# Retention and a routed expert layer in one kernel: four positions of k and v to a packet, chunks of 128 positions on 32 partitions, a mask built by VectorE, and a shifted start in the order model

## The chip, the cores and the metric

The kernel runs on one core of a Trainium2 chip. The metric is the device time of one execution in microseconds, lower is better. Engines are named as in the profile: PE is TensorE (PEld its weight loads), DVE is VectorE, ACT is ScalarE, POOL is GpSimd and SP is SyncE, which here only issues transfers.

## The reference

Eight heads of decayed attention (retention) over 8 sequences of 576 positions, then a layer of eight experts of which each row takes two:

```python
scores = scale * np.matmul(q, k.transpose(0, 1, 3, 2))
gamma = 1.0 - 2.0 ** (-5.0 - np.arange(H))
Dmat = np.where(rel >= 0, gamma[:, None, None] ** rel[None, :, :], 0.0)
attn_out = np.matmul(scores * Dmat[None], v)          # (8, 8, 576, 64)
x = attn_out.transpose(0, 2, 1, 3).reshape(4608, 512)
noisy_logits = x @ w_gate + np.log1p(np.exp(x @ w_noise)) * noise
...
h = np.maximum(x[mask] @ w1[e], 0.0)
out[mask] += top2_w[mask, k, None] * (h @ w2[e])
```

q, k and v are 8 x 8 x 576 x 64 in float32, w1 is 8 x 512 x 1024, w2 is 8 x 1024 x 512.

## The kernel before

**The attention part.** The work is cut into 16 units. A unit is one sequence and four heads; four units make a group `bp` of two sequences. Of the 576 positions the first 512 belong to the unit, and the 64 of the end (the "tail") are done once for each group. The decay is put into q and v by tables (`tab`, `tabq`), so that a chunk of positions needs only a mask of zeros and ones, and what earlier chunks give comes through a state, the sum of k times v over them. For each unit the steps are: `load` (q, k, v from HBM into float32 tiles), `cast` (scale to bf16: k on ACT, q and v on POOL or DVE), `tr` (eight transposes each of k and q on PE, copied back by ACT or DVE), `scores` (k times q inside each of four chunks of 128 positions, evicted by DVE through the mask), `states` (the four running states, evicted into a block-diagonal tile `tb`), and `out_` (the part inside the chunk, `intra`, and the part from the states, `inter`, evicted into `xT`, which holds the rows of x transposed).

**How positions lie.** k and v are loaded in two halves of 256 positions, and in each half partition p holds the positions 2p and 2p+1, so one row of a packet is 2 x 64 numbers of 4 bytes, 512 bytes. A chunk then covers 64 partitions. `scores` and `intra` make 16 matmuls for each pair of heads, with 64 partitions of operand and 64 columns of weights, so that four of them stand side by side in the array. `states` makes 32 matmuls: 16 over 64 partitions and 16 over 128. The transfer of k covers 4 to 16 heads, two transfers for k and two for v each time; from the second group on they bring the data of two units at once. q comes in packets of 2048 bytes, the tail's in packets of 256 bytes.

**The routing and the experts.** After each group, `tail` and `route` compute logits, the two best experts and a place for each row, and write x in rows to HBM (`xd`). The rows are gathered from there for the experts (POOL, indirect transfers), multiplied by w1 and w2 on PE, and scattered to the output (POOL). Some blocks of rows are final before all groups are routed: these "early tiles" (`up`, L1101, and `second`, L1189) are run between the units. All other blocks go through `wide` (L1127) and `second` when the attention is over. The weights of the first three experts come through POOL's transfers, those of the other five through SP's.

**What sets the order.** Nothing runs in the order of the code. `record` lists the operations with their tiles, and `Plan.run` goes through a model with a cost for each operation, takes the one that can start first, and gives it the tiles; each engine's instructions are then written out in that order and run strictly in it. The numbers in the calls of `pl.op` are these costs. SP's loads go through `inp`, which lets a load go only after the load five before it has landed. Where the model sees PE idle before an operation that takes a PSUM tile, `warm` puts matmuls of no use into that tile beforehand (L298), `o.fill` of them, to keep PE at work. They run on the identity and the mask and so need both. Of the eight PSUM tiles the attention may hold seven.

## Time and profile before

| what | us |
|---|---|
| median of 3 runs | 424.81 |
| lowest and highest run | 424.1, 427.77 |
| profiled execution, its own time | 423.66 |
| its span, first to last instruction | 422.1 |
| PE busy in the span | 380.5 |
| ACT, POOL, DVE busy | 265.2, 289.5, 157.8 |
| transfers over the span | 95.92 MB, mean 227 GB/s |

The page of the profile gives busy times by engine, the span in 40 slices, transfers by queue, and groups of instructions by line. Beside it stand answers about the trace: busy times in stretches (columns: stretch, its length, then the busy us and the number of instructions of each engine, the granted clock of PE as a share, the busy share of the 16 DMA engines, and GB/s), instructions in order of time (start, duration, engine, line, operation, tiles, count), and groups of instructions by shape. A DMA share can be over 1 where transfers of two queues overlap on an engine.

### The profile page before, as it was taken

How to read it: one execution, taken by the hardware profiler on the slowest of the kernel's cores; microseconds unless marked ns; L12 is line 12 of the kernel's file. 1: busy time of each engine (PE TensorE's matmuls, PEld its weight loads, DVE VectorE, ACT ScalarE, POOL GpSimd, SP SyncE). 2: the span in 40 equal slices, each digit the busy share in tenths (PEclk: the TensorE clock that was granted, in tenths of full speed). 3: DMA queues.
4: the chain of work that ended last, by engine and by line, in shares of the span. 5: the costliest groups of instructions: out<-in, count | busy, mean ns of one | idle time of the engine just before them, and what ended most of it. 6: DMA issues, size and time to landing. Idle time of an engine off the chain costs nothing. (4 is left out here: it accounts for less than half of the span.)

```text
span 422.1 us, 11266 instructions
## 1 busy us (share of the span) xinstructions
PE 380.5 (90%) x4418; PEld 243.4 (58%) x4418; DVE 157.8 (37%) x459; ACT 265.2 (63%) x459; POOL 289.5 (69%) x314
## 2 busy tenths in 40 slices
PE   4996774986998888999999999999999999999992
PEld 3875654875876666666566644554554454454451
DVE  4645489688858859201232412021121100000001
ACT  2797674983987776556666756655755754555550
POOL 8774594793498827666477677776776786783673
PEclk9999895998999999999999999999999999999998
DMA  7996999999999999943668899999999999787595
GB/s 229 310 250 156 287 315 268 299 288 228 266 318 174 268 206 277 388 143 115 219 222 299 299 199 239 300 236 292 324 224 309 200 119 153 140 117 115 67 136 96
DMA packets 105177, 95.92 MB, mean 227 GB/s; under 512 B 42015, under 2 KB 82464, under 8 KB 105122
## 3 DMA queue, kind: packets, MB, share of 16 engines
q1 hardware_dynamic: 87298, 59.33, 50.4%
q0 software_dynamic: 17824, 35.85, 41.6%
q8 instruction: 35, 0.57, 0.5%
q14 instruction: 20, 0.16, 0.2%
HBM read 72.71 MB, written 26.36 MB: 235 GB/s over the span
## 5 line engine op out<-in xcount | busy, mean ns | idle before, releaser
L1189 PE MATMUL ps<-W,half 128*128 128x512 bf16 x576 | 185.9, 380 | 0.8 <-ACT half L290 0.4
L1127 PE MATMUL ps<-big,W 128*128 128x512 bf16 (+4 forms) x640 | 181.5, 329 | 0.0
L1110 ACT ACTIVATE half<-ps 128x512 bf16<-128x512 f32 (+5 forms) x190 | 94.8, 504 | 97.2 <-PE ps L1127 76.6
L1024 POOL DMA_INDIRECT xg<-xd,xi x80 | 82.7, 1033 | 56.4 <-issue 19.6
L1233 POOL DMA_INDIRECT out_dram<-half,xg x74 | 95.0, 1284 | 32.3 <-issue 14.2
L1189 PEld LDWEIGHTS <-half 128*128 128x128 bf16 x576 | 55.6, 98 | 61.7 <-issue 0.8
L1127 PEld LDWEIGHTS <-W 128*128 128x128 bf16 x640 | 62.5, 98 | 47.8 <-issue 1.0
L1229 DVE TENSOR_SCALAR half<-ps,xg 128x512 f32<-128x512 f32 (+1 forms) x22 | 13.8, 627 | 101.4 <-PE ps L1199 54.8
L1227 ACT ACTIVATE half<-ps,xg 128x512 f32<-128x512 f32 (+1 forms) x57 | 38.1, 668 | 13.1 <-PE ps L1189 12.5
L589 DVE TENSOR_TENSOR half<-ps,mask 128x512 bf16<-128x512 f32 x64 | 40.0, 682 | 12.3 <-PE ps L581 11.6
L290 ACT ACTIVATE half<-ps 128x1024 bf16<-128x1024 bf16 (+1 forms) x36 | 34.8, 988 | 10.0 <-PE ps L556 4.9
L1101 PE MATMUL ps<-half,W 128*128 128x256 bf16 (+1 forms) x288 | 29.5, 257 | 4.6 <-DMA W<-in_moe_w_dram 3.2
L1101 PEld LDWEIGHTS <-W 128*128 128x128 bf16 x288 | 23.9, 98 | 8.2 <-DMA W<-in_moe_w_dram 3.5
L298 PE MATMUL ps<-mask,ident__61 128*128 128x256 bf16 x146 | 21.3, 296 | 7.1 <-POOL mask L361 5.9
L290 ACT ACTIVATE tb<-ps 64x512 bf16<-64x512 f32 x32 | 18.9, 589 | 6.0 <-PE ps L614 5.1
L290 ACT ACTIVATE W<-big 128x1024 bf16<-128x1024 f32 x22 | 22.4, 1048 | 0.0
L534 POOL TENSOR_TENSOR half<-big,tab 128x512 bf16<-128x512 f32 x16 | 16.7, 1051 | 6.7 <-DMA big<-in_v_dram 3.4
L298 PEld LDWEIGHTS <-ident__61 128*128 128x128 bf16 x146 | 14.9, 106 | 9.7 <-POOL ident__61 L353 4.6
L292 DVE CAST W<-big 128x1024 bf16<-128x1024 f32 x18 | 12.1, 716 | 20.4 <-PE ps L1199 15.0
L614 PE MATMUL ps<-half,half 64*64 64x64 bf16 (+2 forms) x512 | 17.2, 214 | 2.7 <-POOL half L534 2.4
L290 ACT ACTIVATE xT<-ps 128x512 bf16<-128x512 f32 (+1 forms) x37 | 18.6, 558 | 0.8 <-PE ps L659 0.5
L534 POOL TENSOR_TENSOR half<-W,tab 128x512 bf16<-128x512 f32 x16 | 17.6, 1109 | 1.8 <-DMA W<-in_v_dram 1.6
(179 smaller groups left out, 433.5 us busy)
## 6 DMA issues: line engine op xcount, KB each, us to landing
big<-in_moe_w_dram SPq DMA_DIRECT2D x40, 512.0 KB
W<-in_moe_w_dram POOLq DMA_DIRECT2D x12, 512.0 KB, 9.6
xd<-xg SPq DMA_DIRECT2D x16, 264.0 KB
W<-in_q_dram SPq DMA_DIRECT2D x16, 256.0 KB
big<-in_k_dram SPq DMA_DIRECT2D x8, 512.0 KB
big<-in_v_dram SPq DMA_DIRECT2D x8, 512.0 KB
big<-in_q_dram SPq DMA_DIRECT2D x16, 256.0 KB
W<-in_k_dram SPq DMA_DIRECT2D x6, 512.0 KB
```

Of the source, the lines that this page charges most:

```text
L290: self.nc.scalar.activation(out, in_, Act.Copy)
L298: self.nc.tensor.matmul(b.t[:, :2 * P], lhsT=ident, rhs=mask.rearrange("p r x -> p (r x)"), start=True, stop=True, skip_group_check=True)
L534: self.eng(e).tensor_tensor(o, i, t, Alu.mult)
L589: nc.vector.tensor_tensor(S.t.bitcast(BF16).rearrange("p (h c x) -> p h c x", h=2, c=2)[:, h], p[h].t.rearrange("p (c x) -> p c x", c=2), ...
L614: nc.tensor.matmul(o[h * HD:(h + 1) * HD, hp, n, :], lhsT=kk[:k, r, c, y], rhs=vv[:k, r, c, y].unsqueeze(1).to_broadcast([k, n.stop - n.st ...
L1024: ins = nc.gpsimd.indirect_dma_start(out=x.t[:n, :], out_offset=None, in_=self.xd[:rows, :], in_offset=IOff(ap=xi.t[:n, h:h + 1], axis=0), ...
L1101: nc.tensor.matmul(pv()[:, f2, :], lhsT=w.t[:, o:o + P], rhs=xv()[:, di, :n], start=(di == 0), stop=(di == KD - 1))
L1110: self.nc.scalar.activation(o, i, Act.Relu)
L1127: self.mm = nc.tensor.matmul(p.t[:, :n], lhsT=w.t[:, o:o + P], rhs=xv()[:, di, :n], start=(di == 0), stop=(di == KD - 1))
L1189: self.mm = self.nc.tensor.matmul(po.t, lhsT=hv[:, c:c + P], rhs=self.W[e].t[:, o:o + DM], start=(f == 0), stop=(f == KF - 1))
L1227: nc.scalar.activation(y.t[:n, c], x, Act.Copy, scale=g()[:n])
L1233: ins = nc.gpsimd.indirect_dma_start(out=self.out[:, :], out_offset=IOff(ap=ix()[:n], axis=0), in_=y.t[:n, :], in_offset=None, bounds_chec ...
```

## The change

**Loads.** Partition p now holds the four positions 4p to 4p+3 of k and v, so a row of a packet is 1024 bytes, and each unit has one transfer of 512 KB for k and one for v. The two transfers of q for each unit stay. A raw tile holds two units.

**Chunks on 32 partitions.** A chunk of 128 positions covers 32 partitions. `scores` and `intra` make 32 matmuls for each pair of heads, with 32 columns of weights in the one and 32 partitions of operand in the other, so that eight stand side by side. `states` makes 64 matmuls, of 128, 96, 64 and 32 partitions for the four states. `out_` takes four PSUM tiles where it took two, half filled, and has four evictions of 256 columns where it had two of 512. The cast of k is one operation of 1024 columns on ACT, not two of 512.

**Mask.** `mask` has four planes. POOL writes two index tiles (`row`, `col`), and DVE makes the planes with four comparisons; four selections on POOL go.

**Order model.** SP's first transfer ends `RAMP` = 2.0 us later in the model, all engines start at 1.0 us, long setup operations of POOL take part in the port rule, `warm` fills only after 15 us of the model's time and uses the PSUM tile that has been free longest instead of the operation's own, and some costs are new (`scores` 0.4 to 0.32, `intra` 0.45 to 0.32, `states` 0.9 to 1.2). The order of everything follows from these and from the new operations.

```diff
@@ Plan
+    RAMP = 2.0
...
-        free, dma_free, port, paced = {}, {}, [0.0], 0.0
+        free, dma_free, port, paced = dict.fromkeys(("PE", "ACT", "DVE", "POOL"), 1.0), {"SP": self.RAMP}, [0.0], 0.0
...
-            if e == "PE" and t < self.WARM and o.allocs:
-                x = max([free.get(e, 2.5)] + [y[0] for x, b in taken for y in x])
-                o.fill = max(0, int((t - x - 0.2) * 0.8 / 0.11))
+            if e == "PE" and 15.0 < t < self.WARM:
+                b = min((x for x in self.slots["ps"] if x[1] is None), key=lambda x: x[0], default=None)
+                n = b and int((t - max(free.get(e, 2.5), b[0]) - 0.2) * 0.8 / 0.11)
+                if n and n > 0:
+                    o.fill = b[2], n
@@ setup
-        mask = f("mask", [P, 2, P], BF16)
...
-                    G.affine_select(m, m, pattern=[[1, 4], [4, 2], [8, 16]], base=-r, channel_multiplier=-2,
-                                    compare_op=Alu.is_ge, fill=0.0)
+        mask = f("mask", [P, 4, P], BF16)
...
+        for r in range(4):
+            o("DVE", 0.2, (mask, r), lambda r=r: V.tensor_scalar(mask.t[:, r], col.t, thr.t, float(r), Alu.subtract, Alu.is_ge),
+              -6, r=[col, thr])
@@ load
-            m = slice(u % 4 * 4, 16 if u % 4 == 2 else 8 if bp or u else 4)
-            for c, t in enumerate(self.raw[n]):
...
-                        m, 256 * c:256 * c + 256].rearrange("h (p r) d -> p h (r d)", r=2)),
-                    w, u, 0.22 * (m.stop - m.start))
+            self.inp(lambda e, s=s, t=t, hq=hq: nc.sync.dma_start(
+                out=flat(t)[:, hq * 1024:hq * 1024 + 1024].rearrange("p (h x) -> p h x", h=4),
+                in_=s[:, :512].rearrange("h (p r) d -> p h (r d)", r=4)), [(t, hq)], u, 1.54)
@@ cast
-        for c in range(2):
-            pl.op({"ACT": 0.63}, 0, lambda e, c=c: k(e, c), r=[(rk[c], x4)], w=[(kn, c)], prio=u, port=True)
+        pl.op({"ACT": 1.06}, 0, k, r=[(rk, hq)], w=[kn], prio=u, port=True)
@@ scores
-                for c in range(2):
-                    for r in range(2):
-                        for h in range(2):
...
-                                nc.tensor.matmul(o[h][e * HD:(e + 1) * HD, c, r], lhsT=kt[s, hp, c, r, e, :],
+                for r in range(4):
+                    for h in range(2):
+                        s = slice(h * HD, (h + 1) * HD)
+                        for j in range(4):
+                            nc.tensor.matmul(o[h][j * 32:(j + 1) * 32, r], lhsT=kt[s, hp, r, j, :],
...
-            pl.op("PE", 0.4, pe, r=[K, Q], w=p, prio=u)
+            pl.op("PE", 0.32, pe, r=[K, Q], w=p, prio=u)
@@ states
-            for k, z in ((HD, 1), (P, 0)):
...
-                                nc.tensor.matmul(o[h * HD:(h + 1) * HD, hp, n, :], lhsT=kk[:k, r, c, y],
-                                                 rhs=vv[:k, r, c, y].unsqueeze(1).to_broadcast([k, n.stop - n.start, HD]),
+            for n in (3, 2, 1, 0):
+                k = 32 * n + 32
                 for hp in range(2):
+                    for r in range(4):
+                        for h in range(2):
...
+                            nc.tensor.matmul(o[h * HD:(h + 1) * HD, hp, n, :], lhsT=kk[:k, r, y], rhs=vv[:k, r, y],
...
-        pl.op("PE", 0.9, lambda e, p=p: pe(e, p), r=[kn, vn], w=[p], prio=u)
+        pl.op("PE", 1.2, lambda e, p=p: pe(e, p), r=[kn, vn], w=[p], prio=u)
@@ out_
-        p = [self.psum("att") for e in range(2)]
+        p = [self.psum("att") for j in range(4)]
...
+            for r in range(4):
+                for h in range(2):
+                    for j in range(4):
+                        q = slice(j * 32, (j + 1) * 32)
+                        nc.tensor.matmul(o[j][h * HD:(h + 1) * HD, hp], lhsT=v[q, r, 2 * hp + h, :], rhs=s[q, h, r],
...
-            pl.op({"ACT": 0.6, "DVE": 0.69}, 0, ev, r=[p[e]], w=[(xT, (hq, b, e))], prio=u)
+            pl.op({"ACT": 0.39, "DVE": 0.42}, 0, ev, r=[p[j]], w=[(xT, (hq, b, j))], prio=u)
```

**Where it moves instructions: SP at the start.** SP's first issues before (W0 to W2 are the buffers for raw q, k and v; a row with x2 stands for two issues):

```order
L485 DMA W1_123<-in_k_dram 128x4x128 x2
L475 DMA W0_122<-in_q_dram 64x2x512 x2
L485 DMA W2_124<-in_v_dram 128x4x128 x2
L485 DMA W1_123<-in_k_dram 128x4x128 x2
L475 DMA W0_122<-in_q_dram 64x2x512 x2
```

SP's first issues now:

```order
L484 DMA W1_123<-in_k_dram 128x4x256
L478 DMA W0_122<-in_q_dram 64x2x512 x2
L484 DMA W1_123<-in_v_dram 128x4x256
L484 DMA W1_123<-in_k_dram 128x4x256
L445 DMA noise_159<-in_moe_noise_dram 64x4x32 x2
L449 DMA noise_159<-in_moe_noise_dram 64x4x8
L445 DMA noise_159<-in_moe_noise_dram 64x4x32
L478 DMA W0_122<-in_q_dram 64x2x512 x2
```

Two issues of k and of v have become one each, and four of the six small loads of the noise now stand ahead of the second unit's q.

**SP at the first group's tail.** Before, the loads of the tail (the `half` tiles, 64x8x64) and of the noise stood in turn, after the v of the units 4 and 5 (big2, big3):

```order
L441 DMA noise_156<-in_moe_noise_dram 64x4x32
L485 DMA big3_80<-in_v_dram 128x8x128
L497 DMA half6_88<-in_k_dram 64x8x64
L441 DMA noise_156<-in_moe_noise_dram 64x4x32
L497 DMA half6_88<-in_k_dram 64x8x64
L445 DMA noise_156<-in_moe_noise_dram 64x4x8
L497 DMA half16_98<-in_q_dram 64x8x64
L441 DMA noise_156<-in_moe_noise_dram 64x4x32
L497 DMA half16_98<-in_q_dram 64x8x64
L441 DMA noise_156<-in_moe_noise_dram 64x4x32
L497 DMA half11_93<-in_v_dram 64x8x64 x2
L445 DMA noise_156<-in_moe_noise_dram 64x4x8
```

The same place now, after unit 4's loads (big0, W0, big1):

```order
L484 DMA big1_78<-in_v_dram 128x4x256
L494 DMA half2_84<-in_k_dram 64x8x64 x2
L432 DMA half14_96<-in_moe_w_gate_dram 128x4x8
L432 DMA half14_96<-in_moe_w_noise_dram 128x4x8
L439 DMA xd_57<-half6_88 1x264
L494 DMA half7_89<-in_q_dram 64x8x64 x2
L494 DMA half13_95<-in_v_dram 64x8x64 x2
L484 DMA big0_77<-in_k_dram 128x4x256
```

The six loads of the noise are gone from here; the two loads of the gates' weights and the write of one dummy row, which stood just ahead, have moved in.

More of the change, by code (lines that the diff above doesn't have):

```diff
@@ L245, in run @@
             if o.fill:
-                self.warm([b for b in o.allocs if b.cls == "ps"][0], o.fill)
+                self.warm(*o.fill)
             o.fn(o.on)
@@ L312, in o @@
         def o(e, cost, b, fn, prio, r=()):
-            pl.op(e, cost, lambda e: fn(), r=r, w=[b], prio=prio)
+            pl.op(e, cost, lambda e: fn(), r=r, w=[b], prio=prio, port=e == "POOL" and cost > 0.8)
         pl.op("ACT", 1.3, lambda e: nc.scalar.preload_act_table_set("natural_log_exp_and_others"), prio=-10)
@@ L463, in load @@
         d = self.u[u] = {}
-        if u % 4 == 0:
-            self.raw = {n: [pl.buf("big", "att", 2) if bp % 2 else pl.buf("wkv", "att") for c in range(2)] for n in "kv"}
-        rows = lambda t, m: (t.t.rearrange("p b x -> p (b x)") if t.n == 2 else t.t)[:, m.start * P:m.stop * P].rearrange(
-            "p (h x) -> p h x", x=P)
+        if u % 2 == 0:
+            self.raw = {n: pl.buf("big", "att", 2) if bp % 2 else pl.buf("wkv", "att") for n in "kv"}
+        flat = lambda t: t.t.rearrange("p b x -> p (b x)") if t.n == 2 else t.t
         for n in "kqv":
```

122 lines of the change are left out of this document (48 added, 74 removed).

## Prediction

> **What bounds the kernel now.** First the busy time in stretches of the span, cut where PE's work changes: the start, the first tail, the middle units, the last units with the first early tiles, the early tiles after the last unit, the wide blocks, the end.
>
> ```profile
> core 0: us, PE busy (x) PEld busy (x) DVE busy (x) ACT busy (x) POOL busy (x), PEclk, DMA share, GB/s
> 0.00:30.00 30.00, 22.60 (x451) 18.82 (x453) 15.39 (x110) 18.98 (x29) 24.61 (x64) 1.00 0.95 262
> 30.00:50.00 20.00, 14.72 (x380) 12.19 (x370) 8.82 (x16) 13.96 (x22) 10.03 (x8) 0.93 0.81 214
> 50.00:94.00 44.00, 32.89 (x845) 28.65 (x838) 36.62 (x108) 33.94 (x58) 32.91 (x40) 0.88 1.07 293
> 94.00:147.40 53.40, 45.79 (x977) 36.17 (x977) 43.16 (x91) 37.91 (x64) 37.56 (x40) 0.97 1.08 251
> 147.40:197.00 49.60, 47.12 (x498) 34.03 (x496) 20.20 (x64) 30.68 (x57) 30.24 (x36) 1.00 0.80 237
> 197.00:414.00 217.00, 217.00 (x1297) 113.57 (x1295) 32.84 (x71) 129.77 (x232) 152.09 (x126) 1.00 0.92 207
> ```
>
> From 197 us on PE has no idle at all, and the change touches nothing there; 414 is when it stops. So the end moves by as much as the first wide matmul moves (L1127). Before it are two regimes. Until 94 us the transfers are the limit: the DMA share is 0.95 to 1.07 but for the stretch at 30 to 50 us, while PE is idle for 7.40 + 5.28 + 11.11 = 23.8 of 94 us. PE's busy time there is also flattered by the matmuls that fill waits:
>
> ```profile
> L298 PE MATMUL ps<-mask,ident__61 128*128 128x256 bf16 x146 | 21.3, 296 | 7.1 <-POOL mask L361 5.9 <-ACT xT L290 0.9 <-ACT tb L290 0.3
> ```
>
> From 94 to 197 us PE is idle for 7.6 + 2.5 = 10.1 of 103 us: there it is PE's own work that counts, with POOL, DVE and ACT each at 70 to 80% of the first half of it. The order in time shows what PE does at that border: unit 10's scores, the eleventh L581 group, at 91.5 us, the first early tile (L1101) at 96 us, and the last unit's `inter` (L659) at 147 us.
>
> ```profile
> 91.46 0.64 PE L581 MATMUL ps<-half,half 64*64 64x128 bf16 x32 [0.17 <-ACT half L290]
> ...
> 96.18 0.38 PE L1101 MATMUL ps<-half,W 128*128 128x256 bf16 x2
> ...
> 146.88 0.51 PE L659 MATMUL ps<-half,tb 128*128 128x128 bf16 x6
> ...
> 197.03 0.92 PE L1127 MATMUL ps<-big,W 128*128 128x448 bf16 x4
> ```
>
> So a saving in transfers counts up to about 94 us, and extra matmuls count after it.
>
> **Packets of k and v.** I look for a stretch that holds nearly only packets of 512 bytes, and for one with packets near 1024 bytes. The first is 12.5 to 15 us (loads of k and v); the second is 66 to 67 us, where the writes of `xd` run, 1056 bytes each. Of each the line of the packets:
>
> ```profile
> DMA packets 1448, 0.73 MB, mean 290 GB/s; under 512 B 30, under 2 KB 1448, under 8 KB 1448
> ```
> ```profile
> DMA packets 336, 0.34 MB, mean 337 GB/s; under 512 B 24, under 2 KB 335, under 8 KB 335
> ```
>
> At full use packets of 512 bytes bring 290 GB/s, packets of twice that 337. k and v of the units are 2 x 8 x 8 x 512 x 64 x 4 bytes = 16.8 MB, so 57.9 us become 49.8 us: 8.1 us saved over 16 units, 0.51 us for each. The units 0 to 11 lie in the limited part (unit 10 is begun at 91.5 us, and loads run ahead): 12 x 0.51 = **-6.1 us**. The other four units' 2 us come where PE is nearly full; PE's idle time there is 7.6 us, part of it waits for data, and I take half, **-1 us**. Bounds: 0 if loads there are never awaited, -2 if always. The write of 1056 bytes goes the other way than these loads, so the 337 is an estimate for a read.
>
> The Trainium skill, page "DMA: Bandwidth & Descriptors", section "Why small descriptors are slow (HBM only)", charges a fixed 3 cycles for each packet beside one for each 32 bytes. By it 512 bytes take 19 cycles and 1024 take 35, so the saving would be 3/38 of 57.9 = 4.6 us and the first term -3.4 us (an estimate from that page); the two rows above are 16% apart where the rule has 9%, and the rows are used.
>
> **Small loads at the first tail.** Between 30 and 43 us SP issues small loads of noise and tail in turn, and the DMA share is 0.81 there:
>
> ```profile
> 30.60 1.43 SPq L497 DMA_DIRECT2D half<-in_k_dram  x1
> 32.07 0.74 SPq L441 DMA_DIRECT2D noise<-in_moe_noise_dram  x1
> 32.91 1.41 SPq L497 DMA_DIRECT2D half<-in_k_dram  x1
> 34.37 0.76 SPq L445 DMA_DIRECT2D noise<-in_moe_noise_dram  x1
> ```
>
> The change takes the six noise loads out (0.62 to 1.08 us of SP each, 4.5 us in all: two are quoted here) and puts three others in, the gates' weights and the dummy row, which took 2.09, 0.80 and 0.44 us before:
>
> ```profile
> 23.19 2.09 SPq L428 DMA_DIRECT2D half<-in_moe_w_gate_dram  x1
> 25.32 0.80 SPq L428 DMA_DIRECT2D half<-in_moe_w_noise_dram  x1
> ...
> 27.05 0.44 SPq L435 DMA_DIRECT2D xd<-half  x1
> ...
> 38.18 0.63 SPq L441 DMA_DIRECT2D noise<-in_moe_noise_dram  x1
> ```
>
> 4.5 - 3.3 = **-1 us**. Bounds: 0, and -4.9 us if the stretch fills up, 20 x (1 - 0.81/1.07). At the front the noise loads are hidden by megabytes of k, q and v in flight; if that cover fails they cost their 4.5 us of SP there.
>
> **The matmuls.** One unit in the PE-bound part, in order of time: scores (L581), states (L614), `intra` (L649), `inter`.
>
> ```profile
> 110.53 0.64 PE L581 MATMUL ps<-half,half 64*64 64x128 bf16 x32
> 111.01 0.99 PE L614 MATMUL ps<-half,half 64*64 64x64 bf16 x32
> 111.93 0.64 PE L649 MATMUL ps<-half,half 64*64 64x128 bf16 x32
> 112.50 0.51 PE L659 MATMUL ps<-half,tb 128*128 128x128 bf16 x6
> ```
>
> From start to start: scores 0.48 us for 32, states 0.92, `intra` 0.57. After the change each has 64. For scores and `intra` the columns that stream are doubled but eight matmuls share the array instead of four, so if streaming limits, nothing changes; if each matmul has a fixed price, the time doubles. The tail's matmuls of half the columns tell which. In slices of 20 ns the sixteen of L726 are all running 0.14 us after the first:
>
> ```profile
> 120.32:120.34 0.02, 0.02 (x4) 0.02 (x4) 1.00 0.99 256
> ...
> 120.44:120.46 0.02, 0.02 (x16) 0.02 (x12) 1.00 0.68 179
> ```
>
> (The second slice quoted is the first with x16.) That is 8.8 ns for each, against 0.48/32 = 15 ns for those of 128 columns: the price falls with the columns. I take 8.8 ns as the floor: scores 64 x 8.8 = 0.56 us, +0.08; `intra` 0.57, +0. `states` now streams 64 x 64 = 4096 columns, two matmuls side by side, where it had 16 x 64 + 8 x 192 + 8 x 64 = 3072: 0.92 x 4/3 = 1.23 us, +0.31.
>
> One more price is the change of layout. The sixteen of L726 had started by 120.46, and the next group, over all 128 partitions, starts at 120.57:
>
> ```profile
> 120.32 0.32 PE L726 MATMUL ps<-half,half 64*64 64x64 bf16 x16
> 120.57 0.41 PE L730 MATMUL ps<-half,tb 128*128 128x64 bf16 x8
> ```
>
> So a change of partitions costs 0.11 us. `states` goes through 128 or 96, 64 and 32 partitions where it had 64 and 128, about two more changes: +0.22. Sum +0.6 us for a unit, of it 0.53 in `states`. The Trainium skill, page "TensorEngine Tiling (Array Packing)", section "Key Properties", says that a change of the tiling mode drains TensorE. By that rule, the trace agrees, with 0.11 us.
>
> After 94 us come the scores and states of units 11 to 15: 5 x 0.61 = **+3.1 us**. The first eleven units' share lies in idle PE. Bounds: 0, and with a fixed price scores +0.48, states +0.92 + 0.22 and `intra` (seven units) +0.57 each: 5 x 1.62 + 7 x 0.57 = +12.1 us.
>
> **The rest, at nothing.** Evictions of `out_`: four of 256 columns instead of two of 512, the cast of k one of 1024 instead of two of 512, all on ACT:
>
> ```profile
> L290 ACT ACTIVATE xT<-ps 128x512 bf16<-128x512 f32 x30 | 16.4, 600 | 0.6 <-PE ps L659 0.5
> L518 ACT ACTIVATE half<-big 128x512 bf16<-128x512 f32 x16 | 9.6, 631 | 3.5 <-DMA big<-in_k_dram 3.5
> L290 ACT ACTIVATE xT<-ps 128x256 bf16<-128x256 f32 x7 | 2.3, 379 | 0.2 <-PE ps L730 0.2
> L290 ACT ACTIVATE W<-big 128x1024 bf16<-128x1024 f32 x22 | 22.4, 1048 | 0.0
> ```
>
> 4 x 0.379 - 2 x 0.600 = +0.32 and 1.05 - 1.26 = -0.21, so +0.11 us of ACT for each unit; ACT is idle for 15 of the 53 us from 94 on, which hides it. If all of it showed there: +0.8 us. The mask took POOL 1.35 us at 4.5 us (first row below) and is first needed by an eviction after unit 0's scores (last row), 7 us later; made by DVE it is hidden likewise. At the start 19 filling matmuls hold PE from 5.9 to 9.9 us, ahead of the transposes for unit 0's scores at 13.0; they go, so unit 0 can be some 2 us earlier:
>
> ```profile
> 4.51 1.35 POOL L361 TENSOR_SCALAR_AFFINE_SELECT mask<-mask 64x128 bf16<-64x128 bf16 x4
> ...
> 5.91 4.01 PE L298 MATMUL ps<-mask,ident__61 128*128 128x256 bf16 x19 [5.91 <-POOL mask L361]
> ...
> 13.01 0.65 PE L581 MATMUL ps<-half,half 64*64 64x128 bf16 x32 [0.24 <-ACT half L290]
> ```
>
> From unit 2 on the transfers set the pace again, so I count 0, with bounds of 0 and -2 us.
>
> **Sum.** -6.1 - 1 - 1 + 3.1 = -5.0 us. The profiled execution took 423.66 us (422.1 of span, 1.56 around it) and becomes 418.7. It lies 1.15 us under the median of the runs, 424.81, so the median becomes **419.8 us**.
>
> **Rivals.**
> 1. *Matmuls at a fixed price, slower.* If the many small matmuls keep 15 ns (scores) to 29 ns (states) each, +12.1 us stand against -8.1: 428.8. It decides from the point where the stretch after 94 us loses 8.1 us, some 1.5 us for a unit: (1.97 + 1.5)/192 = 18 ns for a matmul, where I forecast 13. For it: four of eight neighbours write to other PSUM tiles and have their own weights, and no row shows eight side by side. Against: the 8.8 ns. Chance 0.20.
> 2. *The packets don't matter.* The loads are awaited through POOL's and DVE's casts, and if it is these queues that pace the units, only -1 + 3.1 remain: 426.9. For: POOL is busy for 33 of 44 us from 50 on. Against: a DMA share of 1.07 there. Chance 0.10.
> 3. *PSUM.* `out_` needs four of the seven tiles at once, and its evictions take 1.52 us instead of 1.20; if PE waits for that in the seven units after 94 us, 7 x 0.32 = +2.2: 422.0. Chance 0.10.
> 4. *All the gain, no price.* The stretch at 30 to 50 us fills (-4.9), all 8.1 us of packets count, unit 0's start does too (-2), and the matmuls are hidden by half: 424.8 - 15 + 1.5 = 411 at the best, 414 in the middle. Chance 0.18.
>
> My forecast has 0.42.
>
> **How the numbers follow.** About 1% is what a measurement of this kernel can tell from no change: 420.6 and 429.1 are the limits. The forecast's own range, with the bounds of its small terms, is 416.5 to 424; two thirds of it are under 420.6. Faster: 0.28 of the forecast and 0.18 of rival 4, 0.46. Same: 0.14 of the forecast, 0.09 of rival 3 and 0.07 of rival 2, 0.30. Slower: rival 1 reaches from 426 to 433, but with its longer stalls I count it whole, with 0.04 of rivals 2 and 3: 0.24. The range of 412 to 429.5 leaves out the best end of rival 4 and the worse half of rival 1.
>
> **What would show it.** In the changed profile: packets of k and v at 337 GB/s in a stretch full of them; the first L1127 at about 192 us, and from there PE without idle; a unit's scores about 0.56 us from start to start, its states 1.2 to 1.5, its `intra` 0.57; the DMA share at 30 to 50 us above 0.85. If scores or `intra` take 1 us, rival 1 holds; if PE waits for ACT before `out_`, rival 3. A new idle stretch, where one engine waits in the order written for it, would make all of this wrong, like this one of 5.87 us now, where PE stands at a routing table for DVE:
>
> ```profile
> 68.64 1.38 PE L881 MATMUL ps<-oh,olo 128*128 128x80 f16 x18 [5.87 <-DVE keep_t L865]
> ```

## The result, and the profile after

| what | before | after |
|---|---|---|
| median of the runs, us | 424.46 | 473.96 (472.99 to 477.99) |
| ratio | 1 | 1.117, 95% interval 1.108 to 1.126 |
| span of the profiled execution, us | 422.1 | 472.5 |
| first wide matmul, us | 197.03 | 245.65 |
| PE busy until then, us | 163.11 | 189.95 |
| PE idle until then, us | 33.9 | 55.7 |
| of it put down to "issue", us | 2.1 | 33.4 |

The change costs 49.5 us where 5 were expected to be gained. The table's "until then" rows come from one stretch of each trace, 0 to 197 and 0 to 245.65 us. Nearly all of the loss, 48.62 of the 50.4 us between the two spans, lies ahead of the wide blocks; in order of time, the first of them:

```profile
245.65 0.93 PE L1111 MATMUL ps<-big,W 128*128 128x448 bf16 x4
```

Busy times in stretches of the changed kernel, with the columns of before (stretch, length, busy us and instructions of PE, PEld, DVE, ACT, POOL, granted clock, DMA share, GB/s):

```profile
0.00:30.00 30.00, 16.95 (x449) 14.05 (x449) 16.53 (x101) 14.40 (x20) 23.36 (x74) 1.00 0.93 278
30.00:50.00 20.00, 13.89 (x567) 11.90 (x551) 10.13 (x17) 8.91 (x17) 9.95 (x8) 0.84 0.65 194
50.00:94.00 44.00, 33.58 (x918) 28.01 (x925) 25.15 (x65) 23.96 (x41) 23.17 (x24) 0.77 0.79 244
94.00:147.40 53.40, 39.74 (x1225) 32.28 (x1208) 31.36 (x75) 26.58 (x50) 25.56 (x30) 0.82 0.78 193
147.40:197.00 49.60, 38.62 (x1089) 30.59 (x1088) 30.93 (x73) 28.41 (x57) 20.84 (x25) 0.84 0.63 134
0.00:245.65 245.65, 189.95 (x4631) 150.01 (x4631) 132.35 (x391) 132.21 (x235) 134.03 (x196) 0.87 0.75 206
```

From 30 us on nothing is full any more: the transfers fell from 1.07 of their time to 0.79 in the stretch at 50 us, PE is idle for a fifth to a third of every stretch, and its granted clock is 0.77 to 0.84 where it was 0.88 to 1.00. A slower kernel in which no engine has more of its time filled is one in which something waits, and the waits of PE up to 245.65 us (waiting line, what it waited for, us in total, times, longest) name it:

```profile
PE ps L573 <- issue: 10.8, 6, 4.7
PE ps L602 <- issue: 10.3, 5, 3.9
PE ps L635 <- issue: 7.2, 5, 2.9
PE ps L550 <- ACT half L515: 6.5, 1, 6.5
PE ps L751 <- issue: 3.2, 2, 1.6
```

"Issue" means that the trace shows nothing that PE waited for; with two rows of 1.0 and 0.9 us not shown it comes to 33.4 us. The lines are scores (L573), states (L602) and `intra` (L635), the three steps whose matmuls were doubled. In order of time such a wait looks like this:

```profile
24.80 0.36 PE L635 MATMUL ps<-half,half 32*64 32x128 bf16 x19
28.03 0.62 PE L635 MATMUL ps<-half,half 32*64 32x128 bf16 x45 [2.87 <-issue]
28.58 0.51 PE L644 MATMUL ps<-half,tb 128*128 128x128 bf16 x6
28.93 0.82 PE L301 MATMUL ps<-mask,ident__61 128*128 128x256 bf16 x6
29.68 0.77 PE L573 MATMUL ps<-half,half 64*32 64x128 bf16 x64
30.38 0.31 PE L602 MATMUL ps<-half,half 128*64 128x64 bf16 x7
32.31 0.88 PE L602 MATMUL ps<-half,half 128*64 128x64 bf16 x37 [1.61 <-issue]
```

PE stops in the middle of a group, after 19 of 64 matmuls that all read the same tiles, and again after 7 of 64. No semaphore can be the reason there. Two things tell what is. First, the place: counted in PE's written order, where each matmul has a weight load of its own, the waits lie at the instructions 704, 960, 1472, 1728, 1984, 2240, 2494, 3516, 3772, 4028 and on: the distances are multiples of 256, to within the few instructions that a trace can miss. Between the two waits above are 128 matmuls, 256 instructions. Second, the transfers. Queue 8 carries instructions, in packets of 16 KB; on the page, after, then before:

```profile
q8 instruction: 47, 0.77, 0.7%
```
```profile
q8 instruction: 35, 0.57, 0.5%
```

Twelve packets more go with 1505 more matmuls and as many weight loads: 3010 / 256 = 11.8. And each of the waits ends nearly the same time after such a packet. Cut into stretches of 0.25 us, the transfers show one in 25.25 to 25.5 us and the next in 29.25 to 29.5 us; the rows for these two:

```profile
q8 instruction: 1, 0.02, 27.3%
```
```profile
q8 instruction: 1, 0.02, 37.4%
```

PE goes on at 28.03 and 32.31, 2.5 to 3.1 us after the packet; over the twenty such waits it is 2.4 to 3.1 us. The second packet moves 1.2 to 1.5 us after PE entered the block before it, at 28.03. So PE holds the block that it runs and at most the next one, and asks for a further one only when it enters a new block. Twenty such waits make the 33.4 us; before had three, of 0.41, 0.76 and 0.85 us, 1278 instructions apart both times (5 x 256, but for one matmul).

The Trainium skill, page "Runtime: NRT & Kernel Launch", section "Instruction fetch mechanics", describes such blocks of 256 instructions, fetched one ahead through a DMA queue of the engine's own, and calls the cost of a block's end mostly hidden. The blocks agree with the trace; the cost is hidden in the kernel before (2.1 us) and not in this one (33.4 us).

How long a fetch takes goes with what else moves. For some block ends: when PE entered the block (counted as above), when the next packet of queue 8 moved, and what moved between the two.

```
kernel   entered   packet   later by   GB/s   mean bytes of a packet
after     36.31    37.48     1.17        0      -
after     63.08    64.22     1.14        0      -
after    115.25   116.40     1.15        0      -
before    25.81    27.57     1.76      281    366
before    30.69    32.91     2.22      287    435
after     21.61    25.46     3.85      358   1140
after     45.41    49.25     3.84      371   1194
after     51.88    56.06     4.18      359   1158
before   114.99   118.98     3.99      335    834
after    133.10   135.25     2.15      292   1377
```

With nothing else moving it is close to 1.15 us each time. Beside loads it is more, but the last two rows say that neither the rate nor the size of the packets settles it alone.

From one such wait's end to the next it is 3.7 us where no loads run (115.25 to 118.97) and 6.2 to 6.8 us beside loads (93.71 to 99.91, 45.41 to 51.88, 137.65 to 144.40): that is what a block costs when PE has run dry. Whoever runs through 128 small matmuls faster than that waits for the rest. Scores and states of one unit are 128 matmuls and take 2.07 us where nothing disturbs them:

```profile
70.61 0.78 PE L573 MATMUL ps<-half,half 64*32 64x128 bf16 x64
71.32 1.43 PE L602 MATMUL ps<-half,half 128*64 128x64 bf16 x64
72.68 0.51 PE L550 MATMUL ps<-ident__61,half 128*128 128x128 bf16 x6
```

### The profile page after: what moved, and what is told of

Read it like the earlier page. It is cut to its first block, busy times and chain, and to the rows that moved or that the text cites. A ratio compares the mean times of both kernels' runs of the same rounds, so it can differ in the third digit from the quotient of the medians.

```text
span 472.5 us, 14303 instructions
## 1 busy us (share of the span) xinstructions
PE 407.1 (86%) x5923; PEld 263.6 (56%) x5923; DVE 167.3 (35%) x463; ACT 260.3 (55%) x466; POOL 287.8 (61%) x323
## 4 chain that ended last, share of the span: by engine, by line
PE 73%; DVE 12%; issue 9%; POOL 2%; ACT 2%; POOLq 0%; DVEq 0%
PE ps L1173 23%; PE ps L1111 22%; PE ps L602 5%; PE ps L1085 3%; PE ps L635 3%; PE ps L573 3%; POOL out_dram L1217 2%; DVE olo L858 2%; PE ps L301 2%; PE ps L644 2%; PE ps L892 2%; PE ps L1030 2%; PE ps L544 2%; PE ps L550 2%; PE ps L1183 1%
## 5 line engine op out<-in xcount | busy, mean ns | idle before, releaser
L1213 DVE TENSOR_SCALAR half<-ps,xg 64x256 f32<-64x256 f32 (+1 forms) x22 | 13.3, 603 | 102.5 <-PE ps L1183 54.9
L1211 ACT ACTIVATE half<-ps,xg 128x512 f32<-128x512 f32 (+1 forms) x57 | 38.4, 676 | 11.8 <-PE ps L1173 11.2
L602 PE MATMUL ps<-half,half 32*64 32x64 bf16 (+3 forms) x1024 | 27.4, 208 | 10.3 <-issue 10.3
L293 ACT ACTIVATE half<-ps 128x1024 bf16<-128x1024 bf16 (+1 forms) x31 | 29.9, 987 | 8.6 <-PE ps L544 5.1
L293 ACT ACTIVATE xT<-ps 128x256 bf16<-128x256 f32 x65 | 21.0, 384 | 23.7 <-PE ps L635 19.4
L602 PEld LDWEIGHTS <-half 32*64 32x64 bf16 (+3 forms) x1024 | 23.2, 120 | 14.6 <-issue 12.0
L573 PE MATMUL ps<-half,half 64*32 64x128 bf16 x1024 | 15.0, 235 | 12.6 <-issue 10.8
L635 PE MATMUL ps<-half,half 32*64 32x128 bf16 x1024 | 16.9, 262 | 8.0 <-issue 7.2
L295 DVE CAST W<-big 128x1024 bf16<-128x1024 f32 x21 | 14.3, 731 | 26.2 <-PE ps L1183 15.9
L825 POOL TENSOR_TENSOR ub<-MM,bnd 128x144 f32<-128x144 bf16 x4 | 1.8, 454 | 30.3 <-DVE MM L787 30.3
L573 PEld LDWEIGHTS <-half 64*32 64x32 bf16 x1024 | 10.7, 95 | 17.0 <-issue 16.1
```

The source lines that it names most:

```text
L293: self.nc.scalar.activation(out, in_, Act.Copy)
L573: nc.tensor.matmul(o[h][j * 32:(j + 1) * 32, r], lhsT=kt[s, hp, r, j, :], rhs=qt[s, hp, :, 16 * j:16 * j + 16], start=(r == 0), stop=(r == 3),
L602: nc.tensor.matmul(o[h * HD:(h + 1) * HD, hp, n, :], lhsT=kk[:k, r, y], rhs=vv[:k, r, y], start=(n == 3 and hp == 0 and r == 0), stop=(n = ...
L635: nc.tensor.matmul(o[j][h * HD:(h + 1) * HD, hp], lhsT=v[q, r, 2 * hp + h, :], rhs=s[q, h, r], start=(hp == 0 and r == 0), stop=(hp == 1 a ...
L1211: nc.scalar.activation(y.t[:n, c], x, Act.Copy, scale=g()[:n])
```

## The experiments

Three theories stood at the start: (1) PE runs out of instructions, a block at a time; (2) small matmuls are dear in the array; (3) the new order and the new loads make the engines wait. The runs of the first set (the first four below) were taken where the kernel before took 424.87 us. The others, in two sets, were taken where it took 442.55 and 445.45 us; there only the ratio to before is compared. In the last set (experiments 6, 7, 8 and 12) before's own runs lie between 441.96 and 456.06 us, and neither for its four results nor for that of experiment 9 is "slower" or "same" on record, only "unclear"; their ratios are good to about a hundredth. Ranges in us in these texts are meant for a kernel before of 424.9 us.

**1. The changed kernel with before's number of matmuls** (`a_few`). Loads, order model, mask, PSUM tiles and evictions stay as changed; chunks are joined in pairs, so the output is not the reference's, q is multiplied by zero, and FIRST[6] is 203 to fit the early blocks to the routing that this gives. 4431 matmuls where the changed kernel has 5967 and before 4462.

```diff
-                        for j in range(4):
-                            nc.tensor.matmul(o[h][j * 32:(j + 1) * 32, r], lhsT=kt[s, hp, r, j, :],
+                        for j in (0, 2):
+                            nc.tensor.matmul(o[h][j * 32:j * 32 + HD, r], lhsT=kt[s, hp, r, j:j + 2, :],
...
-            for n in (3, 2, 1, 0):
-                k = 32 * n + 32
+            for k, z in ((HD, 1), (P, 0)):
...
-                    for j in range(4):
-                        q = slice(j * 32, (j + 1) * 32)
+                    for j in (0, 2):
+                        q = slice(j * 32, j * 32 + HD)
```

> The changed kernel with the number of matmuls of before: scores and intra over 64 partitions or 64 columns (16 for a pair of heads), states in 32 matmuls with the same streamed columns as before; q is multiplied by zero, so the attention's result is left out, and expert 6 has six more places. Loads, packets, evictions, PSUM use, order model and order stay those of the changed kernel. Theory 1 (PE runs out of instructions, a block of 256 at a time): the waits without a releaser inside the groups go, 33 us of them, and the time falls to 415 to 428. Theory 2 (small matmuls are dear in the array): it falls as well, to 440 or below, but then splitting matmuls without changing the array's layout costs nothing. Theory 3 (the new order and loads make the engines wait): it stays at 465 to 475.

Measured: 427.37 us, 1.0066 times before (1.0028 to 1.0105). With the extra matmuls the loss goes, and of the 33.4 us of issue 10.3 are left. Theory 3 falls: nearly the whole new order and all the new loads are still in it.

**2. The kernel before, with its matmuls cut in two** (`b_split`): the same loads, layout, order and streamed columns, 1536 matmuls more.

```diff
-                            for e in range(2):
-                                j = 2 * c + e
-                                nc.tensor.matmul(o[h][e * HD:(e + 1) * HD, c, r], lhsT=kt[s, hp, c, r, e, :],
-                                                 rhs=qt[s, hp, :, 16 * j:16 * j + 16],
+                            for z in range(2):
+                                for e in range(2):
+                                    j = 2 * c + e
+                                    nc.tensor.matmul(o[h][e * HD:(e + 1) * HD, c, r, 4 * z:4 * z + 4], lhsT=kt[s, hp, c, r, e, :],
+                                                     rhs=qt[s, hp, 4 * z:4 * z + 4, 16 * j:16 * j + 16],
...
```

> The kernel before with its matmuls of scores and intra each cut into two of 64 columns, and those of states into pieces of 32 or 64, so that each step has 64 instead of 32 and the same columns stream in the same layout of four tiles; nothing else is changed and the result is the same. Theory 1: PE waits at every 256th instruction as the changed kernel does, 450 to 475 us. Theory 2: the array's layout is that of before, 424 to 430. Theory 3: 424 to 430.

Measured: 467.04 us, 1.098 times before (1.094 to 1.102): the kernel before becomes as slow as the changed one by nothing but more matmuls. Its waits up to 250 us show the same sign, now at scores (L582), `intra` (L657) and the transposes (L556):

```profile
PE ps L582 <- issue: 13.0, 6, 3.9
PE ps L657 <- issue: 10.2, 5, 3.3
PE ps L556 <- issue: 6.2, 3, 2.7
```

In all 35.0 us of issue, 33 more than before, of the 42.2 us that it lost; the waits lie 256 instructions or a multiple apart, and queue 8 has 47 packets. What theory 2 would need, a group of small matmuls that runs slowly, isn't there: the 64 of L582 that were undisturbed in experiment 6 took from 30.34 us to the next group at 30.92, 9 ns each (rows there).

**3. The kernel before with packets of 1024 bytes** (`b_pk1k`). k and v come four positions to a partition, one half of the heads in each transfer; bytes, matmuls and layout stay, so positions are permuted, and FIRST[6] is 203.

```diff
...
                     in_=self.src[n][2 * bp:2 * bp + 2].rearrange("b h s d -> (b h) s d")[
-                        m, 256 * c:256 * c + 256].rearrange("h (p r) d -> p h (r d)", r=2)),
+                        m2, :512].rearrange("h (p r) d -> p h (r d)", r=4)),
```

> The kernel before with k and v in packets of 1024 bytes: the same number of transfers and bytes to the same places, but positions and heads lie elsewhere, so the attention's result is another one; expert 6 has six more places. The term of the prediction for packets alone is -6 to -8 us: 416 to 419. If the loads don't set the pace, 423 to 425.

Measured: 422.63 us, 0.994 times before (0.992 to 0.996): 2.2 us gained. The packets do what the prediction said of them; the transfers at 12.5 to 15 us, where before had 290 GB/s:

```profile
DMA packets 898, 0.89 MB, mean 358 GB/s; under 512 B 25, under 2 KB 898, under 8 KB 898
```

The gain can be followed by the unit whose scores begin: 67.82 and 73.38 us for two units that began at 69.95 and 76.05 before, then 84.14 and 93.76 for the next two, at 82.90 and 91.46 before. Between lie three waits of the same kind, of 1.41, 1.64 and 1.12 us at 75.6, 82.1 and 89.3 us, 254 instructions apart both times (256, but for one matmul): data that comes earlier lets PE run into the end of its block, and 4.2 us go there, more than the 2.7 us won by then. The waits of PE up to 250 us put down to issue have risen from 2.1 to 6.4 us:

```profile
PE ps L553 <- issue: 2.8, 2, 1.6
PE ps L584 <- issue: 1.4, 1, 1.4
PE ps L911 <- issue: 0.9, 1, 0.9
PE ps L1104 <- issue: 0.7, 1, 0.7
PE ps L662 <- issue: 0.6, 1, 0.6
```

**4. The kernel before with the order model's edits and the mask on DVE** (`b_plan`), neither loads nor matmuls changed.

```diff
+    RAMP = 2.0
...
-        free, dma_free, port, paced = {}, {}, [0.0], 0.0
+        free, dma_free, port, paced = dict.fromkeys(("PE", "ACT", "DVE", "POOL"), 1.0), {"SP": self.RAMP}, [0.0], 0.0
...
-                self.warm([b for b in o.allocs if b.cls == "ps"][0], o.fill)
+                self.warm(*o.fill)
...
+            o("DVE", 0.2, (mask, r), lambda r=r: V.tensor_scalar(mask.t[:, r], col.t, thr.t, float(r), Alu.subtract, Alu.is_ge),
```

> The kernel before with the order model's edits (first transfer 2 us later, engines at 1 us, filling after 15 us and into the tile free longest, the port rule in the setup) and the mask built by DVE, but its own loads, packets and chunks. Theories 1 and 2: these parts are nearly free, 420 to 428. Theory 3: a good part of the loss is here, 435 or more.

Measured: 427.72 us, 1.008 times before (1.005 to 1.012). Packets and order together, -0.6% and +0.8%, leave +0.2%; experiment 1 has +0.66%, with new evictions beside them.

**5. A control for experiment 1** (`a_zero`): the changed kernel with q times zero and FIRST[6] = 203, all its matmuls kept.

```diff
...
-        o("ACT", 0.25, tabq, lambda: nc.scalar.activation(tabq.t, tabq.t, Act.Exp), -8)
+        o("ACT", 0.25, tabq, lambda: nc.scalar.activation(tabq.t, tabq.t, Act.Copy, scale=0.0), -8)
```

> A control for the run with before's number of matmuls: the changed kernel with all its 1505 extra matmuls, and only the two side edits of that run (q is multiplied by zero, and one number of the table FIRST is 203, which fits the early blocks to the routing that this data gives). Theory 1 (PE runs out of instructions, a block of 256 at a time): nothing that matters is changed, 466 to 482 us, with 28 to 37 us of idle PE put down to issue. Rival: it was the zeros (less power, a higher granted clock) or the routing that brought the time back, then 425 to 450 us here too.

Measured: 484.3 us, 1.092 times before (1.085 to 1.100), with 34.3 us of issue (some 6 us of it in short stops of another kind, for which see the last section). Neither the zeros nor the routing brought the time back in experiment 1. That the ratio is 1.092 and not 1.117 goes with the time of before there, 442.55 instead of 424.46 us: the difference to before is 41.8 us there and 49.5 us here; the rest of that difference was not looked into.

**6. The same cut, the first eleven units alone** (`b_split_first`), and **7. the last five alone** (`b_split_last`). The first tests the prediction's sentence that the first eleven units' share lies in idle PE.

```diff
-                            for z in range(2):
+                            for z, w in ((0, 4), (1, 4)) if u < 11 else ((0, 8),):
...
```

> The kernel before with the matmuls of scores, states and intra cut in two for the units 0 to 10 alone (1056 more by these cuts; the streamed columns stay). The prediction put these units' share into the idle time of PE: then 1.00 to 1.01 times before. Theory 1 (PE runs out of instructions): a block of 256 still has to be fetched while PE stands ready, and the later idle time does not give it back, because what the units do next waits for it: in the run with all units cut 14 of 35 us of issue lay before 94 us, so 1.03 to 1.07 times before.

> The same cut for the units 11 to 15 alone (480 more by the cuts). If the loss of the run with all units cut (9.8%) lies where PE has no idle time, as the prediction thought of extra matmuls: 1.08 to 1.10 here, all of it. Theory 1: its share by the issue idle after 94 us, 21 of 35 us: 1.03 to 1.06.

Measured: 1.058 (1.051 to 1.065) for the first eleven, 1.032 (1.025 to 1.039) for the last five; 5.8% + 3.2% = 9.0%, the 9.8% of all of them but for the errors. Two of the four runs of the first cut lie near 470 us; the other two, 462.55 and 467.31, are 4 to 5% over before, so 5.8% is on the high side. The loss is there in both parts, whether PE has idle time there or not: 1056 extra matmuls cost 4 to 6%, 480 cost 3.2%. The first wait of the cut in the first eleven, at 24.76 us, stands before the transposes and puts off all that follows in that unit:

```profile
24.76 0.56 PE L556 MATMUL ps<-ident__61,half 128*128 128x128 bf16 x7 [2.71 <-issue]
...
30.34 0.76 PE L582 MATMUL ps<-half,half 64*64 64x64 bf16 x64
30.92 0.69 PE L623 MATMUL ps<-half,half 64*64 64x32 bf16 x32
...
33.60 0.25 PE L664 MATMUL ps<-half,half 64*64 64x64 bf16 x6
35.99 0.22 PE L664 MATMUL ps<-half,half 64*64 64x64 bf16 x4 [2.13 <-issue]
```

**8. Only states with before's number** (`a_few_states`): the changed kernel, 512 matmuls fewer.

```diff
-            for n in (3, 2, 1, 0):
-                k = 32 * n + 32
+            for k, z in ((HD, 1), (P, 0)):
...
```

> The changed kernel with before's number of matmuls in states alone (512 fewer; the states then come out for pairs of chunks, and q is multiplied by zero, FIRST as in the control). Theory 1: what counts is how many instructions stand close together, so a third of the extra matmuls gone takes a third of the loss or somewhat more: 1.05 to 1.08 times before. If states' own time (four partition counts, more columns) made the loss: 1.01 to 1.03. If it plays no part: 1.085 to 1.10, as in the control.

Measured: 1.068 times before (1.062 to 1.074), between the 1.092 of the control and the 1.007 of experiment 1. A third of the extra matmuls is 26% of the loss, (9.2 - 6.8) / 9.2. So states' own layout and columns, which are gone here too, make about a quarter of the loss at the most.

**9. As many small matmuls where blocks last long** (`b_wide`): before, the experts' matmuls cut in two halves of columns, 1216 more.

```diff
-                self.mm = nc.tensor.matmul(p.t[:, :n], lhsT=w.t[:, o:o + P], rhs=xv()[:, di, :n],
-                                           start=(di == 0), stop=(di == KD - 1))
+                for x, y in ((0, n // 2), (n // 2, n)):
+                    self.mm = nc.tensor.matmul(p.t[:, x:y], lhsT=w.t[:, o:o + P], rhs=xv()[:, di, x:y],
+                                               start=(di == 0 and x == 0), stop=(di == KD - 1 and y == n),
...
```

> The kernel before, with the experts' matmuls of up to 512 columns (the wide blocks and the second product) cut into two halves of columns: 1216 matmuls more, nearly as many as the 1346 of the run that cut the units' matmuls, but where a block of 256 instructions lasts 128 x 0.1 us = 13 us. Theory 1: PE runs dry only where 256 instructions last less than their fetch, about 4 to 6.5 us, so nothing is lost: 422 to 429 us, no idle put down to issue after 200 us. Theory 2, each small matmul has its own price wherever it stands: 42 us / 1346 = 31 ns each in that run, so 1216 x 31 ns = 38 us, 455 to 467 us; at half that price 440 to 446.

The 1346 in that text counted experiment 2 only up to a certain time; the cut makes 1536, so theory 2's price is 27 ns and its sum 33 us. Measured: 1.026 times before (1.019 to 1.033), 11 us: neither theory's range. The first wide matmul is at 218.28 us, against 212.62 in experiment 10, which is before but for the mask: 5.7 us are lost ahead of it, where 120 of the added matmuls belong to the early tiles. From there on the profiled execution is 8.5 us longer than that of experiment 10; 4.5 of these are idle time of PE in the groups of the wide blocks, in 250 to 400 us:

```profile
L1128 PE MATMUL ps<-big,W 128*128 128x256 bf16 (+3 forms) x814 | 122.4, 252 | 2.9 <-issue 2.7
L1192 PE MATMUL ps<-W,half 128*128 128x256 bf16 x583 | 104.2, 273 | 1.6 <-issue 1.5
```

These stops are short, 0.2 to 0.5 us with one of 0.9, often one 0.7 us after the other, and not at block ends: they are of the kind in the last section. So no block end is waited for in the wide blocks, as theory 1 has it, and theory 2's 33 us are not there; that the cut costs nothing, as theory 1 forecast, is wrong by 11 us, whose cause this run does not settle.

**10. The mask alone on DVE** (`b_mask`), the index tiles and the comparisons of experiment 4 in the kernel before.

> The kernel before with the mask alone made by DVE (two index tiles on POOL, two comparisons). The run with the order model's edits and this mask together took 0.8% more than before. If the order model's edits did that: 423 to 426 us here, or a little under before, since the filling matmuls and unit 0 wait for the mask. If the mask did it: 427 to 429 us.

Measured: 1.000 times before (0.997 to 1.004). The mask is hidden, as forecast, and the 0.8% of experiment 4 belong to the order model.

**11. Fewer loads in flight** (`a_shallow`): two of SP's loads where the changed kernel has five, filling matmuls three at most.

```diff
...
-        self.inps.append(self.pl.op("SP", 0.55, fn, w=t, prio=prio, dma=dma, after=self.inps[-5:-4]))
+        self.inps.append(self.pl.op("SP", 0.55, fn, w=t, prio=prio, dma=dma, after=self.inps[-2:-1]))
```

> The changed kernel with at most two of SP's loads in flight instead of five (and at most three filling matmuls in a row, so that their number stays: 112 for 115). In the changed kernel a block of 256 PE instructions is fetched 0.7 to 1.4 us after PE enters the block before it where loads move under 100 GB/s, and 3.3 to 4.1 us after where they move over 280. Theory 1a, the fetch stands behind the packets of the loads: with fewer of them in flight it comes after 2.5 us or less also where loads run, and the idle time of PE put down to issue falls from 33 us to 22 or less; the time falls with it unless the loads themselves get slower, 455 to 478 us. Theory 1b, the fetch takes its time whatever the loads do, and the two went together by chance: 3.3 to 4.1 us as before, 28 to 38 us of issue, 470 to 490 us.

Measured: 506.83 us, 1.143 times before (1.136 to 1.150), with 26.9 us of issue. The loads got slower, so the time lies above both ranges, and the issue lies between the two. Some fetches were as late as before. For one: PE entered a block at 76.26 us, and queue 8's next packet moved in 80.0 to 80.25, 3.7 us later, while loads ran at 308 GB/s.

```profile
74.62 0.60 PE L602 MATMUL ps<-half,half 128*64 128x64 bf16 x26
76.26 1.02 PE L602 MATMUL ps<-half,half 96*64 96x64 bf16 x38 [1.04 <-issue]
```
```profile
q8 instruction: 1, 0.02, 26.4%
```

Others came sooner than every row of the table above with 300 GB/s or more: for the blocks entered at 50.62 and 99.72 us the packet moved at 52.43 and 100.87, 1.8 and 1.2 us later, beside some 330 GB/s. Theory 1a as it was put, with 2.5 us at most, falls, and so does 1b, by which the loads don't matter. The two groups that the text above gives for the changed kernel are too neat as well: the table has 2.15 us at 292 GB/s, and a block entered at 103.64 us had its packet 2.1 us later beside 63 GB/s. Two loads of 512 KB are still a megabyte, 2.9 us at 360 GB/s, so it stays open whether the fetch waits behind the loads' packets, and whether their size matters; loads of less than that were not tried.

**12. Tell the order model** (`a_cost`): the changed kernel with costs for the three steps that stand for their fetch.

```diff
-            pl.op("PE", 0.32, pe, r=[K, Q], w=p, prio=u)
+            pl.op("PE", 1.0, pe, r=[K, Q], w=p, prio=u)
...
-        pl.op("PE", 1.2, lambda e, p=p: pe(e, p), r=[kn, vn], w=[p], prio=u)
+        pl.op("PE", 2.1, lambda e, p=p: pe(e, p), r=[kn, vn], w=[p], prio=u)
```

> The changed kernel with the order model's costs of the three steps set to what their instructions take to fetch (scores and intra 0.32 to 1.0 for a half, states 1.2 to 2.1); nothing else is edited, the order follows. If the order can spread the small matmuls among other work: 1.03 to 1.07 times before and under 20 us of issue. If a unit has too many instructions for any order (some 200 matmuls in 8 us, 1.6 blocks of 4 to 6.5 us): 1.08 to 1.14.

Measured: 1.097 times before (1.089 to 1.105), no better than the control, with 38 us of issue, some of it in the short stops of the last section. This order, at least, doesn't spread the blocks.

| kernel | matmuls | packets of queue 8 | issue, us | times before |
|---|---|---|---|---|
| before | 4462 | 35 | 2.1 | 1 |
| 3, packets of 1024 bytes | 4462 | 35 | 6.4 | 0.994 |
| 1, changed, few matmuls | 4431 | 35 | 10.3 | 1.007 |
| 2, before, cut | 5998 | 47 | 35.0 | 1.098 |
| changed | 5967 | 47 | 33.4 | 1.117 |

No kernel here that computes the reference is faster than before.

## Why the prediction was wrong

It gave 419.8 us and a range to 429.5; the time is 473.96. Of its cases none had this wait. It named a new idle stretch as a sign of being wrong, and one came, but it thought of one engine that waits for another.

**The step that failed** is the one on the matmuls: "After 94 us come the scores and states of units 11 to 15: 5 x 0.61 = +3.1 us. The first eleven units' share lies in idle PE." It priced a matmul by the columns that it streams and took PE's idle time as room for more of them. Both halves are wrong in the same way: an instruction has to be fetched before it can use idle time. By their fetch the 3010 added instructions are 11.8 blocks of 3.7 to 6.8 us, 44 to 80 us (an estimate from the block ends above), part of it behind other work. Experiment 6 shows the second half alone: 4 to 6% lost with the cut in the first eleven units, where 0 to 1% was expected of the prediction's reading.

**What the array takes** was sized fairly well. Undisturbed, from start to start, a unit's scores take 0.71 us (0.56 forecast), its states 1.36 (1.45 with the changes of layout), its `intra` 0.69 (0.57): +0.79 us for a unit where +0.61 was forecast. That is 14 ns for a matmul on average, and rival 1 was to decide from 18 ns on. So rival 1, which was right that small matmuls cost more, had the wrong mechanism: 11 to 21 ns each in the array, but 30 us of idle PE around them.

**The sum of the 48.6 us** up to the first wide matmul: issue +31.3; all other idle time 22.3 us where it was 31.8, -9.5; PE busy +26.8. Of this, 16 units at the measured +0.79 make 12.6 us, and 31 filling matmuls fewer take off 4.5 (before had 146 of them in 21.3 us):

```profile
L301 PE MATMUL ps<-mask,ident__61 128*128 128x256 bf16 x115 | 18.4, 308 | 0.3 <-ACT tb L293 0.3
```

The rest has the size of the clock's share: before's scores take 0.86 us from start to start where the granted clock is 0.50 (at 49.10 us) and 0.45 where it is 1.00 (at 24.76 us). The row of the kernel before for the same part, in the columns of the stretches:

```profile
0.00:197.00 197.00, 163.11 (x3122) 129.85 (x3123) 124.18 (x387) 135.47 (x227) 135.34 (x186) 0.96 0.96 255
```

163.11 + 12.6 - 4.5 = 171.2 us of work at the mean granted clock before, 0.96, is 171.2 x 0.96 / 0.87 = 188.9 us at that of 0.87 (an estimate), and 189.95 were measured. That the lower clock follows from the waits is argued, not tried alone: over the whole execution the clock is 0.93 in the changed kernel and in experiment 2, and 0.98 and 0.99 in before and in experiment 1, where the waits are few. The Trainium skill, page "TensorE: Matmul & The Clock Gate", section "Part 1: The HAM clock gate", has the clock gated down when PE has been idle for a while. The rows agree, with 0.77 to 0.84 in the stretches with most waits.

**Packets**, -6.1 and -1 us: mis-sized in the total, -2.2 us in experiment 3. The rate rose more than forecast, 358 GB/s for 337, and the units did come 2 to 3 us earlier for a while; then the same wait took it. So rival 2 (the packets don't matter) has the size, but by another cause than POOL's and DVE's queues.

**Small loads at the first tail**, -1 us: the sign by which it was to be known, a DMA share above 0.85 at 30 to 50 us, did not come: it is 0.65, in a stretch that holds waits of PE as well. The term can't be read apart from the rest.

**The rest, at nothing.** The mask is right (experiment 10). ACT's evictions are too: no row of PE's waits names the eviction of `xT`, and rival 3 (PSUM) has nothing for it either. The order model, which the prediction counted only by the transfers that it moves and the filling matmuls that go, costs 0.8% by itself (experiment 4 less experiment 10).

**What held besides**: from the first wide matmul to the end it is 226.9 us where it was 225.1, so the end moved by little more than that matmul did, 50.4 and 48.6 us in the two profiled executions.

## What to carry to other kernels

Count a kernel's TensorE instructions as well as its columns: each matmul is two (itself and its weight load), 128 matmuls are a block, and here a block cost 3.7 us with quiet queues and 6.2 to 6.8 us under loads, so pieces that get through 128 matmuls in 2 us wait for their instructions however idle the engine is elsewhere. In a trace the sign is an engine that stops in the middle of a group with no one to wait for, at distances of 256 instructions, 2.4 to 3.1 us after a packet of the instruction queue. A change that makes transfers better by making matmuls smaller has to be priced in both.

## What the runs showed that was not expected

In the changed kernel the fetch of a block moved some 1.15 us after it could be asked for when nothing else moved, and 3.8 to 4.2 us after beside loads at 358 to 371 GB/s; where PE waited for it, it was 2.4 to 3.1 us from there to the block's first instruction in both cases. What sets the time beside loads stays open (experiment 11).

A faster load can lose its gain to the fetch without any change on PE (experiment 3: 4.2 us of such waits against 2.7 us won).

Where the kernel before took 442.55 or 445.45 us, PE shows another kind of stop in the kernels of both sets: a few instructions, then up to 0.5 us of nothing, some 0.73 us from one to the next; in the one below the granted clock falls from 1.00 to 0.50 meanwhile. One of them in experiment 10, in order of time:

```profile
112.48 0.22 PE L616 MATMUL ps<-half,half 64*64 64x64 bf16 x2 [0.49 <-issue]
113.18 0.39 PE L616 MATMUL ps<-half,half 64*64 64x64 bf16 x2 [0.48 <-issue]
113.91 0.48 PE L616 MATMUL ps<-half,half 128*64 128x192 bf16 x4 [0.34 <-issue]
114.63 0.59 PE L616 MATMUL ps<-half,half 128*64 128x64 bf16 x6 [0.24 <-issue]
```

These too are put down to issue, but only two to six matmuls lie between them, and one packet of queue 8 moves in all that time (113 to 113.5 us) where each block end has its own; what makes them was not looked into.
